# Expert layers issued in the order of a list scheduler inside the kernel, dense tails run in the next expert, float64 weights decoded in place

## The chip, the cores and the metric

The kernel runs on one core of a Trainium2 chip. The metric is device time in microseconds (us) of one launch; smaller is better. Engines are named as the profile names them: PE (TensorE matmuls, its weight loads PEld), DVE (VectorE), ACT (ScalarE), POOL (GpSimd), and SP, whose queue issues most DMAs.

## What is computed

Windowed attention, then a greedy assignment of 2304 tokens to 8 experts of 288 places each, two layers of the token's expert, and two dense layers:

```python
scores = np.where(mask, q @ k.T / 8 - slope * rel, -1e9)     # mask: 0 <= rel < 128; 4 batches, 8 heads, 576 rows, 64 wide
x = softmax(scores) @ v                                      # as 2304 rows of 512
for idx in np.argsort(-(x @ w_gate).flatten()):              # highest logit first
    tok, e = idx // 8, idx % 8
    if assigned[tok] < 0 and counts[e] < 288:
        assigned[tok] = e; counts[e] += 1
x[mask_e] = np.maximum(x[mask_e] @ w1[e], 0) @ w2[e]         # w1: 512x1024, w2: 1024x512, float32
h = x @ w_in                                                 # w_in: 512x2048, w_out: 2048x512, float64
out = np.maximum(0.01 * h, h) @ w_out
```

The assignment can be made one expert at a time: among the tokens left, the expert that is the first to be asked by 288 of them closes with these.

## The kernel before

Every float32 operand of a matmul is cut into two parts of a narrower form, high and low (`hh` and `hl`, `xh` and `xl`, `w1h` and `w1l`, and so on), and a product is three matmuls: high by high, low by high, high by low. ScalarE makes the high part by a copy; the low one is a subtraction on DVE or POOL (`Weights.split`).

Up to about 178.8 us the kernel runs the attention, and decodes 14 of the 16 tiles of `w_in` beside it. Float64 weights come as pairs of 32-bit words in a buffer `raw` (3 of them): ScalarE scales the upper words into a tile `wz`, DVE shifts the lower words in place and joins the two in `wz` (`Weights.fixed`), and the split into high and low reads `wz`. `raw` is free once the last joining step has read it. Then comes the assignment of the first expert (`Route.phase(0)`), and the loop over the eight experts:

- `X.gather` fetches the expert's 288 rows of x by three indirect DMAs from POOL's queue, and `X.turn` transposes them on PE into `xh` and `xl` (96 rows by three, two PSUM banks at a time).
- `X.moe` has 8 steps. A step loads its parts of w1 and w2 (SP queue), splits them, does 12 matmuls of the first layer into a bank `h`, the relu (ScalarE `hh`, DVE `hl`), and, one step later (lag 1), 12 of the second layer into four banks `acc`. At the end `acc` becomes `yh` and `yl`.
- `X.dense` has 16 steps of the same kind with resident weights and lag 2. Its leaky relu takes two ScalarE passes, a POOL subtraction (`lk`), a ScalarE copy (`hh`) and a POOL subtraction (`hl`). At the end `acc` is copied, transposed back on PE and scattered to the output rows by three indirect DMAs.

Beside them runs the assignment of the coming experts. For expert 1 it is `Route.phase(1)`, comparisons on DVE counted by matmuls. For experts 2 to 7 (`Late`) it is on DVE alone: a search of 11 rounds (`search`), each a scan of 1152 logits on each partition (`below`) and eight short steps on its result; `found` and `tokens`, which send a `line` of running counts through DRAM; and `listed`, three scans of that line that give `idx`, the rows to gather. `prepare` and `fetch` write the next candidates to DRAM and read them back.

The order of the work around all this was set by hand, in tables: at which dense step the next rows are gathered (`GATHER`) and turned (`TURN`), beside which steps a round of the search runs (`SEARCH`, `AHEAD`), which weights POOL splits (`POOL_W`), at which steps a dense tile is decoded (`IN_MOE`, `IN_DENSE`). `tc.issue_after(...)` ties a piece behind another instruction. On top of it the compiler's own scheduler moves instructions on each engine. At run time every engine works its queue in order.

Of the kernel before, what the change touches and what calls it, by code (L numbers as in the profile page):

```python
# [32 lines left out]
# engines of copies out of PSUM: A ScalarE, D VectorE; for weights by block, for an even and an odd unit  # L33
# [25 lines left out]
# shifts of the search by rows: digits of 3 bits, but the first of 2  # L59
# [40 lines left out]
class Attention:  # L100
    """Windowed attention of head pairs; leaves the rows of x in DRAM and the gate logits in SBUF.
# [298 lines left out]
class Route:  # L400
# [85 lines left out]
    def phase(s, i, ps, tb):  # L486
# [3 lines left out]
        def pst(shape):  # L490
            return ps.tile(shape, FT, name="T", bufs=tb)
# [16 lines left out]
        for rd, (bits, sh) in enumerate(rounds):  # L508
# [636 lines left out]
```

## Time and profile before

| | us |
|---|---|
| median of 3 runs | 962.7 |
| the runs | 963.95, 960.68, 962.70 |
| span of the profiled execution (the profile gives no other time of its own) | 959.1 |
| PE busy in it | 857.1 (89%) |
| DVE busy | 655.0 (68%) |
| ACT, POOL busy | 457.7 (48%), 389.8 (41%) |

The median is 3.6 us above the profiled span. Shares of busy time are means over stages with different limits, so the profile is read by stretches below. A stretch's line gives its length, then for each engine its busy time and the number of instructions, then the clock that was granted to PE as a share of 2.4 GHz, and the DMA engines' share and GB/s. A line of the timeline gives start, duration, engine, source line, operation, what is written and read, and in brackets the idle time of the engine before it with what ended it.

### The profile page before, as it was taken

What the parts mean: (1) busy time and instruction counts of PE and PEld (TensorE: products, weight loads), DVE (VectorE), ACT (ScalarE), POOL (GpSimd) and SP (SyncE); (2) the same over time, 40 slices, a digit from 0 to 9 for tenths busy, and PEclk for the clock granted to TensorE, in tenths of its full rate; (3) what the DMA queues carried; (4) which work ended last, traced back from release to release, by engine and by line L of the source; (5) the groups of instructions that cost most, each with busy time, mean ns of one, the idle gap of its engine ahead of it and who ended that gap; (6) DMA issues with size and microseconds to landing.
All of it is one profiled execution on the core that took longest, in us unless ns stands there. A gap on an engine that the chain in (4) does not pass through costs nothing.

```text
span 959.1 us, 18148 instructions
## 1 busy us (share of the span) xinstructions
PE 857.1 (89%) x6496; PEld 786.5 (82%) x6496; DVE 655.0 (68%) x1848; ACT 457.7 (48%) x1225; POOL 389.8 (41%) x430
## 2 busy tenths in 40 slices
PE   6999999669888989698988898889888999999995
PEld 5766766559778989598988898889888989999995
DVE  5789999768997797869767875886588525614200
ACT  5899888635545433343244324432443254344432
POOL 0021121210547635374467345734573441452353
PEclk9999999869988999799999998999899999999998
DMA  7567663146345301440404040404040312204000
GB/s 185 147 179 182 174 171 109 56 135 206 103 128 148 116 1 25 114 135 1 113 26 136 1 113 26 135 1 114 26 135 7 96 54 91 86 25 135 1 1 25
DMA packets 127578, 87.80 MB, mean 92 GB/s; under 512 B 70720, under 2 KB 112192, under 8 KB 127488
## 3 DMA queue, kind: packets, MB, share of 16 engines
q1 hardware_dynamic: 122944, 72.49, 27.3%
q0 software_dynamic: 4544, 14.16, 4.9%
q8 instruction: 51, 0.84, 0.3%
q14 instruction: 39, 0.32, 0.1%
HBM read 76.72 MB, written 9.91 MB: 90 GB/s over the span
## 4 chain that ended last, share of the span: by engine, by line
PE 36%; DVE 28%; issue 17%; POOL 10%; ACT 5%; DMA 3%; SPq 0%; POOLq 0%; DVEq 0%; ACTq 0%
PE acc L911 10%; PE h L921 8%; DVE below L678 6%; POOL lk L950 5%; PE X L281 4%; POOL hl L955 4%; PE T L247 3%; PE S L198 3%; DVE f L687 3%; ACT hh L954 2%; DVE th L700 2%; DVE wz L833 2%; PE T L158 1%; POOL xrow L866 1%; DVE next L676 1%
## 5 line engine op out<-in xcount | busy, mean ns | idle before, releaser
L950 POOL TENSOR_TENSOR lk<-lr,lk 128x288 f32<-128x288 f32 x128 | 108.5, 848 | 206.0 <-ACT lk L949 176.3
L955 POOL TENSOR_TENSOR hl<-lk,hh 128x288 fp32r<-128x288 f32 x128 | 106.0, 828 | 74.3 <-ACT hh L954 74.3
L954 ACT ACTIVATE hh<-lk 128x288 fp32r<-128x288 f32 x128 | 56.9, 444 | 165.5 <-POOL lk L950 165.3
L911 PE MATMUL acc<-hh,woh 128*128 128x288 f32 x512 | 97.7, 305 | 18.2 <-ACT hh L954 18.2
L911 PE MATMUL acc<-hh,wol 128*128 128x288 f32 x512 | 97.0, 304 | 0.0
L911 PE MATMUL acc<-hl,woh 128*128 128x288 f32 x512 | 96.5, 304 | 0.0
L911 PEld LDWEIGHTS acc<-hh,woh 128*128 128x128 f32 x512 | 79.4, 195 | 19.4 <-ACT hh L954 19.4
L921 PE MATMUL h<-yh,wih 128*128 128x288 f32 x512 | 94.8, 307 | 0.0
L921 PE MATMUL h<-yl,wih 128*128 128x288 f32 x512 | 92.2, 299 | 0.0
L948 ACT ACTIVATE lr<-h 128x288 f32<-128x288 f32 x128 | 52.0, 406 | 82.3 <-PE h L921 81.3
L921 PE MATMUL h<-yh,wil 128*128 128x288 f32 x512 | 89.9, 297 | 0.0
L921 PEld LDWEIGHTS h<-yh,wih 128*128 128x128 f32 x512 | 79.2, 196 | 0.9
L911 PEld LDWEIGHTS acc<-hl,woh 128*128 128x128 f32 x512 | 79.4, 196 | 0.4 <-POOL hl L955 0.3
L911 PEld LDWEIGHTS acc<-hh,wol 128*128 128x128 f32 x512 | 79.6, 195 | 0.1
L921 PEld LDWEIGHTS h<-yh,wil 128*128 128x128 f32 x512 | 76.4, 192 | 0.0
L921 PEld LDWEIGHTS h<-yl,wih 128*128 128x128 f32 x512 | 76.3, 190 | 0.0
L678 DVE TENSOR_SCALAR_CACHE_REDUCE below<-bc,th 128x1152 uint8<-128x1152 f32 x50 | 70.3, 1406 | 0.0
L795 DVE TENSOR_SCALAR_CACHE_REDUCE below<-lb,place 96x2304 uint8<-96x2304 f16 x18 | 47.0, 2608 | 34.2 <-DMA lb<-line 33.7
L232 ACT ACTIVATE P<-sc,mn 128x256 f32<-128x256 f32 (+1 forms) x144 | 68.3, 477 | 3.8 <-DVE mn L230 3.2
L911 PE MATMUL acc<-hl,w2h 128*128 128x288 f32 x256 | 52.9, 313 | 16.9 <-DVE hl L938 16.7
L810 POOL TENSOR_TENSOR w1l<-raw,w1h 128x512 fp32r<-128x512 f32 x36 | 47.7, 1325 | 32.4 <-ACT w1h L809 29.9
L809 ACT ACTIVATE w2h<-raw 128x512 fp32r<-128x512 f32 x64 | 40.3, 630 | 41.6 <-PE acc L911 30.7
(289 smaller groups left out, 1976.0 us busy)
## 6 DMA issues: line engine op xcount, KB each, us to landing
raw<-in_moe_w_dram SPq DMA_DIRECT2D x128, 256.0 KB, 3.0
raw<-in_moe_w_in_dram SPq DMA_DIRECT2D x16, 512.0 KB, 4.5
raw<-in_moe_w_out_dram SPq DMA_DIRECT2D x16, 512.0 KB, 4.1
qn<-in_q_dram SPq DMA_DIRECT2D x32, 128.0 KB, 2.5
kn<-in_k_dram SPq DMA_DIRECT2D x32, 128.0 KB, 3.0
vn<-in_v_dram SPq DMA_DIRECT2D x32, 128.0 KB, 2.4
xd<-rows POOLq DMA_DIRECT2D x16, 256.0 KB
bc<-cand SPq DMA_DIRECT2D x5, 576.0 KB, 5.4
```

The costliest lines, as they stand in the source:

```text
L232: nc.scalar.activation(P[:, x, w], sc[:, x, w], AF.Exp, bias=mn[:, x:x + 1], scale=-1.0, accum_out=acc)
L281: nc.tensor.matmul(xp[64 * h2:64 * h2 + 64, 128 * kb:128 * kb + n], V[:, kb, h2, :], t[:, n * h2:n * h2 + n], start=kb == 0, stop=kb == 3, ...
L678: V.tensor_scalar(junk, s.bc, s.thr.bitcast(FT), None, op0=OP.is_lt, op1=OP.add, accum_out=s.cl[:, 0:1])
L795: V.tensor_scalar(junk, lb, s.place[:, x:x + 1], None, op0=OP.is_lt, op1=OP.add, accum_out=at[:, x:x + 1])
L809: s.nc.scalar.activation(hi, raw, AF.Copy)
L810: (s.nc.gpsimd if pool else s.nc.vector).tensor_tensor(lo, raw, hi.bitcast(FT), op=OP.subtract)
L911: nc.tensor.matmul(acc[d], w[:, 128 * d:128 * d + 128], v, start=f == 0 and n == 0, stop=last and n == 2)
L921: nc.tensor.matmul(p, w[:, k], v[:, k], start=n == 0 and k == 0, stop=n == 2 and k == 3)
L948: nc.scalar.activation(r, p, AF.Relu)
L950: nc.gpsimd.tensor_tensor(t, r, t, op=OP.subtract)
L954: s.hh.append(nc.scalar.activation(hh, t, AF.Copy))
L955: s.hl.append((nc.gpsimd if pool else nc.vector).tensor_tensor(hl, t, hh.bitcast(FT), op=OP.subtract))
```

## The change

The loop over the experts no longer issues instructions. It writes down operations for a planner, `Plan`: each has an engine, a duration written in the code, a function that issues its instructions, the operations it comes after with a latency, the buffers it takes and gives back, and the time by which PE's train wants it. `Plan.run` then takes operations one at a time: for every engine it looks at those whose inputs and buffers are there, takes the engine on which something can start first, and on it the one wanted soonest; it issues it and sets the engine's clock on. The assignment is a thread of such operations (generators that `yield` engine and duration), which is wanted 60 or 80 us ahead of the list's use and otherwise fills gaps. `tc.manual_schedule()` keeps the order as issued. Operations with `alt` may go to DVE in place of POOL when they would be late. The hand-written tables are gone.

Besides, the expert layers have lag 2 from expert 1 on; the three last second-layer steps of the dense layers are handed on (`rest`) and issued among the next expert's first steps, and its output transposes after them; the turn uses one PSUM bank of its own (`tx`), the assignment and the outputs another (`to`); a one-element memset on POOL stands ahead of each scatter; float64 weights are decoded in `raw` itself, without `wz`, so that `raw` is held until the last split; `idx` and `ei` have five buffers instead of two; and the last tile of `w_in` is split ahead of the first assignment. In the attention nothing else is changed.

```diff
 class Weights:
-    nc.scalar.activation(z, high.bitcast(FT), AF.Copy, scale=2.0 ** -112)
-    nc.vector.tensor_scalar(low, low, 29, None, op0=OP.logical_shift_right)
-    nc.vector.scalar_tensor_tensor(x, x, 3, low, op0=OP.logical_shift_left, op1=OP.bitwise_or)
-    nc.vector.scalar_tensor_tensor(x, high, -2147483648, x, op0=OP.bitwise_and, op1=OP.bitwise_or)
+    def scale(e): nc.scalar.activation(v["high"].bitcast(FT), v["high"].bitcast(FT), AF.Copy, scale=2.0 ** -112)
+    def high(e): nc.vector.tensor_scalar(v["low"], v["low"], 29, None, op0=OP.logical_shift_right)
+    def both(e): nc.vector.scalar_tensor_tensor(v["low"], v["high"], 3, v["low"], op0=OP.logical_shift_left, op1=OP.bitwise_or)
+    def sign(e): nc.vector.scalar_tensor_tensor(v["low"], v["high"], -2147483648, v["low"], op0=OP.bitwise_and, op1=OP.bitwise_or)
+    def upper(e): nc.scalar.activation(hi, v["v"], AF.Copy)
+    def lower(e): (nc.gpsimd if e == "P" else nc.vector).tensor_tensor(lo, v["v"], hi.bitcast(FT), op=OP.subtract)
...
+class Plan:
+    LAT = 0.12
+    SLACK = 1.2
+    AHEAD = 9.0
+    WINDOW = {"T": 0.1, "V": 0.3, "A": 0.3, "P": 0.3, "S": 0.1}
...
+    def run(s, there, threads):
...
+            for o in s.ready:
+                t = s.start(o)
+                if t is None or o.eng == "T" and not o.owner and o.late > s.order[0].late + s.AHEAD:
+                    continue
+                for e in o.eng + (o.alt[0] if o.alt else ""):
+                    at = max(t, s.free[e])
+                    if e == o.eng or o.late - at < 1.0:
+                        found.setdefault(e, []).append((at, o.late, o))
+            e = min(found, key=lambda e: min(c[0] for c in found[e]))
+            first = min(c[0] for c in found[e])
+            at, _, o = min((c for c in found[e] if c[0] <= first + s.WINDOW[e]), key=lambda c: c[1])
...
+            o.end = s.free[e] = at + dur
+            if o.fn:
+                o.fn(e)
...
 class Experts:
+    MM, TR = .1325, .09
...
+    def fixed(s, src, shape, hi, lo):
+        raw = Hold("raw")
+        load = p("S", .5, fn[0], acq=[raw])
+        scale = p("A", .68, fn[1], [(load, 4.5)])
+        high = p("V", .45, fn[2], [(load, 4.5)])
+        both = p("V", .7, fn[3], [scale, high])
+        sign = p("V", .7, fn[4], [both])
+        upper = p("A", .63, fn[5], [sign])
+        lower = p("P", 1.32, fn[6], [upper], rel=[raw], alt=("V", .7))
...
+    def expert(s, i, x, reg, before):
+        for f in range(F1 // 128):
+            w = s.moe_weights(i, f, reg)
+            c, h, t = s.first(w[0][3], w[0][:2], w[0][2], lambda: (x["xh"], x["xl"]), (x["h"], x["l"]), x["hold"])
+            part = s.relu(c, h, t)
+            if f in (0, 1) and before:
+                before.pop(0)()
+            if f == 1 and i:
+                s.outputs()
+            pend.append((f, w[1], part))
+            if f >= 2 or (f == 1 and not i):
+                g, w2, pt = pend.pop(0)
+                s.second(g, False, w2[3], w2[:2], w2[2], pt, acc)
...
+        while pend:
+            rest.append(lambda p=pend.pop(0): s.dense_second(*p, out))
...
+    def route():
+        yield from R.second(first, ps, chosen[1], listed[1], ei, idx)
+        yield from LR.begin(first)
...
+        for i in range(2, NE):
+            if not last:
+                yield from LR.search()
+                yield from LR.found()
+            yield from LR.expert(last, chosen[i], ei)
+            yield from LR.tokens(last)
+            if i < NE - 2:
+                yield from LR.prepare()
+                yield from LR.fetch()
+            yield from LR.listed(listed[i], idx)
+    with tc.manual_schedule():
+        plan.run([listed[0], chosen[0], X.none], [Thread(route(), [(listed[1], 60.0)] + [(e, 80.0) for e in listed[2:]])])
```

What the planner makes of it is shown at three places, as the order of instructions on an engine. A row there is a source line, an operation, what it writes and reads, the size, and how many in a row.

PE between two experts in the middle of the run. Before (`acc<-hl,woh` ends the dense layers, `T<-ident,yh` and `h<-ident,yh` transpose the output, `h<-xh,w1h` begins the next expert):

```order
L911 MATMUL acc<-hl,woh 128x288
L979 MATMUL T<-ident,yh 96x128 x8
L979 MATMUL h<-ident,yh 96x128 x4
L921 MATMUL h<-xh,w1h 128x288 x4
L921 MATMUL h<-xh,w1l 128x288 x4
```

The output was transposed between the last dense matmul and the next expert's first. Now, between experts 2 and 3:

```order
L1280 MATMUL tx<-ident,xrow 128x96 x3
L1373 MATMUL acc<-hh,woh 128x288
L1373 MATMUL acc<-hh,wol 128x288
L1373 MATMUL acc<-hl,woh 128x288
L1354 MATMUL h<-xh,w1h 128x288 x8
L1354 MATMUL h<-xh,w1l 128x288 x8
L1354 MATMUL h<-xl,w1h 128x288 x8
L1373 MATMUL acc<-hh,woh 128x288
L1373 MATMUL acc<-hh,wol 128x288
L1373 MATMUL acc<-hl,woh 128x288
```

Two first-layer groups of the next expert stand ahead of the last dense matmuls; the transposes of the output (`to<-ident,yh`) follow later, one by one among its layers.

DVE where the list of an expert's rows is done (`below,at<-lb` are the scans of the line, `idx` the list, `below,cl<-bc` a scan of the next search, `xl` the low part of turned rows, `hl<-lk` a leaky step's low part). Before:

```order
L795 TENSOR_SCALAR below,at<-lb,place 96x2304 x3
L796 CAST idx<-at 96x3
L882 TENSOR_TENSOR xl<-T,xh 128x288 x4
L678 TENSOR_SCALAR below,cl<-bc,tk 128x1152
L680 STREAM_TRANSPOSE ct<-cl 128x32
```

The next search stood behind the four `xl` of the rows just listed. Now:

```order
L1242 TENSOR_TENSOR hl<-lk,hh 128x288
L1137 TENSOR_SCALAR below,at<-lb,place 96x2304 x3
L1140 CAST idx<-at 96x3
L988 TENSOR_SCALAR below,cl<-bc,tk 128x1152
L1242 TENSOR_TENSOR hl<-lk,hh 128x288
L995 STREAM_TRANSPOSE ct<-cl 128x32
```

The search goes on at once, and the `xl` stand among its later rounds.

SP's queue in the first expert (`in_moe_w_dram` are an expert's weights, `in_moe_w_out_dram` and `in_moe_w_in_dram` the dense ones). Before, the last of the expert's weights and what follows:

```order
L824 DMA raw<-in_moe_w_out_dram 128x1024
L889 ISA
L889 DMA raw<-in_moe_w_dram 128x4x128
L890 ISA
L890 DMA raw<-in_moe_w_dram 128x512
L889 ISA
L889 DMA raw<-in_moe_w_dram 128x4x128
L890 ISA
L890 DMA raw<-in_moe_w_dram 128x512
L824 DMA raw<-in_moe_w_out_dram 128x1024 x8
L824 DMA raw<-in_moe_w_in_dram 128x4x256
```

Some dense tiles were loaded among the expert's weights. Now:

```order
L1306 DMA raw<-in_moe_w_dram 128x4x128
L1309 ISA
L1309 DMA raw<-in_moe_w_dram 128x512
L1177 DMA raw<-in_moe_w_out_dram 128x1024 x3
L1609 TENSOR_LOAD ei
L1609 ISA x2
L1177 DMA raw<-in_moe_w_out_dram 128x1024 x6
L912 DMA flat<-lm 128x4x8
```

Two tiles of `w_out` stand ahead of the expert's weights; the other fourteen and the two of `w_in` come behind all of them.

## Rows read from the trace of the kernel before

**Rows 1.** Stretches of each expert (E0 to E7) and the end.
```profile
208.40:316.00 107.60, 95.20 (x732) 90.69 (x732) 88.84 (x180) 54.82 (x121) 45.36 (x44) 0.91 0.48 140
316.00:414.40 98.40, 86.08 (x605) 83.86 (x604) 79.57 (x229) 36.26 (x85) 51.07 (x53) 0.93 0.23 62
414.40:510.00 95.60, 84.74 (x609) 82.41 (x608) 71.63 (x188) 36.13 (x86) 51.87 (x55) 0.97 0.26 74
510.00:605.40 95.40, 84.58 (x600) 82.72 (x600) 71.19 (x187) 34.95 (x84) 49.65 (x52) 0.94 0.22 64
605.40:700.40 95.00, 84.22 (x598) 82.34 (x597) 70.72 (x188) 34.80 (x84) 50.68 (x53) 0.95 0.24 69
700.40:786.90 86.50, 79.10 (x579) 77.49 (x578) 55.93 (x139) 34.08 (x82) 45.87 (x49) 0.98 0.25 74
786.90:867.00 80.10, 79.02 (x598) 78.22 (x597) 34.45 (x64) 34.97 (x84) 31.55 (x38) 1.00 0.24 73
867.00:947.60 80.60, 80.60 (x608) 80.05 (x607) 16.07 (x29) 32.49 (x77) 29.65 (x36) 1.00 0.09 29
947.60:959.10 11.50, 1.43 (x12) 1.00 (x10) 0.75 (x2) 1.60 (x3) 2.76 (x3) 0.78 0.17 51
```

**Rows 2.** Timeline of PE: a count of E0's assignment, and two dense steps.
```profile
251.80 0.61 PE L518 MATMUL T<-rt_oh,cmp 128*31 128x8 bf16 x18 [1.62 <-DVE cmp L471]
...
686.83 0.69 PE L921 MATMUL h<-yh,wih 128*128 128x288 f32 x4
...
690.01 0.43 PE L921 MATMUL h<-yh,wih 128*128 128x288 f32 x2
```

**Rows 3.** Waits of PE, 208.4 to 947.6: total, times, longest.
```profile
PE acc L911 <- ACT hh L954: 18.2, 5, 4.9
PE acc L911 <- DVE hl L938: 16.7, 16, 2.1
PE T L879 <- DVE xl L882: 10.3, 4, 4.7
PE T L979 <- DVE yh L975: 7.5, 3, 2.5
PE T L879 <- DMA xrow<-xd,idx: 4.4, 1, 4.4
```

**Rows 4.** Timeline of DVE in E2: list scans, turn, three search scans.
```profile
470.11 2.61 DVE L795 TENSOR_SCALAR_CACHE_REDUCE below<-lb,place 96x2304 uint8<-96x2304 f16 x1 [5.34 <-DMA lb<-line]
...
487.75 0.82 DVE L882 TENSOR_TENSOR xl<-T,xh 128x288 fp32r<-128x288 f32 x2 [9.52 <-ACT xh L881]
...
494.49 1.41 DVE L678 TENSOR_SCALAR_CACHE_REDUCE below<-bc,th 128x1152 uint8<-128x1152 f32 x1
...
497.26 1.41 DVE L678 TENSOR_SCALAR_CACHE_REDUCE below<-bc,th 128x1152 uint8<-128x1152 f32 x1
...
500.85 1.41 DVE L678 TENSOR_SCALAR_CACHE_REDUCE below<-bc,th 128x1152 uint8<-128x1152 f32 x1
```

**Rows 5.** Groups of DVE in E2: busy us, mean ns of one.
```profile
L938 DVE SCALAR_TENSOR_TENSOR hl<-h,hh 128x288 fp32r<-128x288 f32 x8 | 3.6, 445 | 1.9 <-issue 1.9
...
L810 DVE TENSOR_TENSOR w1l<-raw,w1h 128x512 fp32r<-128x512 f32 x1 | 0.7, 686 | 0.0
```

**Rows 6.** Timeline of SP's queue: eight tiles of w_out in a row.
```profile
230.27 27.63 SPq L824 DMA_DIRECT2D raw<-in_moe_w_out_dram  x8
```

**Rows 7.** Groups of ACT in E0: strided scale, copy of packed words.
```profile
L830 ACT ACTIVATE wz<-raw 128x512 f32<-128x512 f32 x17 | 11.5, 674 | 8.0 <-DVE wol L810 2.7 <-DMA raw<-in_moe_w_out_dram 2.6 <-DVE wz L832 1.6
L809 ACT ACTIVATE woh<-wz 128x512 fp32r<-128x512 f32 x15 | 9.4, 629 | 7.2 <-DVE wz L833 7.0
```

**Rows 8.** Groups of DVE in E0's expert layers, 208.4 to 238.5.
```profile
L833 DVE SCALAR_TENSOR_TENSOR wz<-raw,wz 128x512 int32<-128x512 int32 x4 | 2.7, 680 | 0.0
```

**Rows 9.** Groups of DVE in E0's dense layers, 238.5 to 316.
```profile
L833 DVE SCALAR_TENSOR_TENSOR wz<-raw,wz 128x512 int32<-128x512 int32 x13 | 15.2, 1169 | 0.0
L832 DVE SCALAR_TENSOR_TENSOR wz<-wz,raw 128x512 int32<-128x512 int32 x13 | 12.1, 933 | 1.7 <-ACT wz L830 1.4
```

More of the change, by code (lines that the diff above doesn't have):

```diff
@@ new lines, in __init__, with pe, copy, minus @@
+        s.at = 9.0
+        s.wi_there, s.wo_there = {}, {}
+    def pe(s, dur, fn, after, **k):
+        o = s.plan.op("T", dur, fn, after, late=s.at, **k)
+        s.at += dur
+        return o
+    def copy(s, e, o, i):
+        if e == "A":
+            s.nc.scalar.activation(o, i, AF.Copy)
+        else:
+            s.nc.vector.tensor_copy(o, i)
+    def minus(s, e, o, a, b):
+        (s.nc.gpsimd if e == "P" else s.nc.vector).tensor_tensor(o, a, b, op=OP.subtract)
+    def warm(s, n):
+        def go(e):
+            for _ in range(n):
+                p = s.ps.tile([128, 512], FT, name="h", bufs=2)
+                s.nc.tensor.matmul(p, s.wih[0][:, 0, :128], s.wih[0][:, 0, :512], start=True, stop=True)
+        s.plan.op("T", 3.8, go, late=0.0)
@@ new lines, in second, with mm, by_part, go @@
+    def second(s, f, last, w, wops, hold_w, part, acc):
+        nc = s.nc
+        def mm(d, n):
+            a, b = w(), part["get"]()
+            x, y = ((0, 0), (1, 0), (0, 1))[n]
+            nc.tensor.matmul(acc["p"][d], a[x][:, 128 * d:128 * d + 128], b[y], start=f == 0 and n == 0, stop=last and n == 2)
+        def by_part(n):
+            def go(e):
+                if f == 0 and n == 0:
+                    acc["p"] = [s.ps.tile([128, CAP], FT, name="acc", bufs=4) for _ in range(4)]
+                for d in range(4):
+                    mm(d, n)
+            return go
+        def by_bank(d):
+            def go(e):
+                for n in range(3):
+                    mm(d, n)
+            return go
+        rel = [part["hold"]] + ([hold_w] if hold_w else [])
+        after = [[wops[0], part["h"]], [wops[1]], [part["l"]]]
+        if last:
+            prev, acc["done"] = acc["prev"], []
+            for d in range(4):
+                prev = [s.pe(3 * s.MM, by_bank(d), sum(after, []) + prev, rel=rel)]
+                acc["done"].append(prev[0])
+        else:
+            prev = acc.get("prev", [])
+            for n in range(3):
+                prev = [s.pe(4 * s.MM, by_part(n), after[n] + prev, rel=rel, acq=acc["hold"] if f == 0 and n == 0 else ())]
+            acc["prev"] = prev
@@ new lines, in tile_attention_moe_mlp, with value @@
+    first = era.enter_context(tc.tile_pool(name="first", bufs=1))
+    LR = Late(tc, keep, dram, R, L)
+    idx, ei = [idx0], [ei0]
+    listed = [plan.op(None, 0.0) for _ in range(NE)]
+    chosen = [plan.op(None, 0.0) for _ in range(NE)]
+    X.warm(8)
+    rest = None
+    for i in range(NE):
+        reg = [None, []]
+        def value(e, i=i, reg=reg):
+            reg[1].append(nc.sync.value_load(ei[i][0:1, 0:1], min_val=0, max_val=NE - 1))
+        reg[0] = plan.op("S", .5, value, [chosen[i]])
+        x = X.turn(i, X.gather(i, [listed[i]], lambda i=i: idx[i]))
+        if i:
+            X.idx_out, X.is_last = (lambda i=i: idx[i - 1]), False
+        rest = X.expert(i, x, reg, rest)
```

869 lines of the change are left out of this document (592 added, 277 removed).

## The prediction

> **What bounds the kernel now.** I read the stretches first, one for each expert's two layers with the two dense layers after them; I call them E0 to E7. TensorE (PE) does the same matmuls in each, yet they last from 107.6 us down to 80.1 [rows 1]. In E6 it is busy for 79.02 of 80.10 us at a granted clock of 1.00, which is 2.4 GHz: that is what an expert costs when nothing holds PE up, and I take 79 as its price. The matmul train says the same: from one first-layer group to the next, 24 matmuls with 288 columns, 686.83 to 690.01, are 3.18 us [rows 2], or 0.1325 each; an expert has 24 blocks of 24 of them, 576, so 76.3 us, and the rest is transposes. E0 also holds the matmuls of the second assignment, 18 in 0.61 us for each of six rounds (one of them in [rows 2]) and some smaller ones, about 6 us: its price is 85.
>
> So the eight stretches should cost 85 + 7 x 79 = 638 us, and cost 739.2 (208.40 to 947.60). The 101 us over that lie in E0 to E5, and the waits of PE tell how [rows 3]: 18.2 us for `hh` of the dense layers, 16.7 for `hl` of the expert layers, 10.3 for `xl` of the turned rows, 7.5 for the copy out of the accumulators, 4.4 for gathered rows. With smaller ones that is some 65 us. The rest is the clock: a stretch at 0.93 spent about 14% of its time at 1.2 GHz, always behind such waits. E6 and E7, with the same layers but hardly any search, have neither. What differs is VectorE (DVE): 88.84 us busy in E0, 79.57 in E1, some 71 in E2 to E4, 34 and 16 in the last two [rows 1]. DVE carries the assignment of tokens, whose chain for one expert has to end before the next expert's rows are gathered. In its timeline a round of the search takes 2.77 us (494.49 to 497.26) or, where a few of its small steps are held up, 3.59 (497.26 to 500.85); DVE then waits 5.34 us for the list's line, and 9.52 us for `xl`, in which it does nothing of the search [rows 4]. The bound is thus PE in E6 and E7, and the assignment in turn with PE in E0 to E5: each waits for the other.
>
> **The change, part by part.**
>
> *Dense tails and transposes moved.* The three last second-layer steps stand behind two first groups of the next expert, and the output transposes among its matmuls. No PE work is added. What goes is the wait for the copy (7.5 us) and for the last `hh` (a part of 18.2). The cover is 24 matmuls at 0.1325, 3.2 us, more than the longest copy wait of 2.5 [rows 3].
>
> *Expert layers at lag 2.* A second-layer group now comes two steps behind its first, so `hl` has 3.2 us more than before; the longest wait for it was 2.1 us [rows 3]. I take the 16.7 us as gone wherever DVE keeps up.
>
> *The search runs on behind the list.* This decides. In the new DVE order the next search follows the list of places directly, where it used to stand behind `xl`; the 9.52 us are filled. But the order also says how much DVE has to do before it may release PE. Between the first `xl` of one turn and that of the next it has 15 search scans in E1, 13 in E2, 12 in E3, 11 in E4 and 4 in E5, where each had 11. DVE is an in-order queue, so these stand before the next turn. From E2's 71.6 us [rows 1], with 3.2 us a round (the mean of 2.77 and 3.59), 0.686 for a weight split and 0.445 for an `hl` [rows 5]:
> E1: 71.6 + 4 rounds (12.8) + 3 splits more (2.1) + the last dense tile's decoding (3.0, four steps of 0.5 to 0.9) + 2 `hl` (0.9) = 90.4, of which a little falls into E0's last steps: 89.
> E2: 71.6 + 2 x 3.2 + 4 x 0.686 + 8 x 0.445 = 84.3: 84.
> E3: 71.6 + 3.2 + 7 x 0.686 + 4 x 0.445 = 81.4: 81.5.
> E4: 71.6 + 9 x 0.686 + 5 x 0.445 = 80.0, with PE's 79 beside it: 81.
> E5 needs 7 rounds fewer, so PE bounds it: 79 and 1.5 for four turns through a single PSUM bank instead of two: 80.5. E6 and E7: 80 each, as now.
>
> *E0: the second assignment beside the expert layers, decoding in place.* DVE's 88.84 us lose 9 weight splits (25 stood on it, by the two orders 16 do now) and two copies, 7.2 us, and gain 7 dense `hl`, 3.2: 84.9, and it starts on the assignment while the first rows are still on their way. The other limit is the three load buffers. A tile now holds its buffer until its last split; before, until the last decoding step. Before, eight tiles in a row left the queue in 27.63 us [rows 6], 3.45 a tile. Now 16 tiles (14 of w_out, 2 of w_in) come behind the expert's weights, from about 232: 16 x 3.45 = 55 to 287, and some 8 to land, decode and split the last, so 295, and the tails after that: E0 ends near 298, at 90 instead of 107.6. In place, every step walks over every other word. Some did before: ScalarE's scale reads strided words in 0.674 us where its copy of packed ones takes 0.629 [rows 7], 7% more, and DVE's last step, strided in one operand, ran in 0.68 undisturbed [rows 8]. A strided split on GpSimd is shown by no row. Its ends are the 7% (0.09 us) and the double of its 1.3 us, for twice the words walked over, which over three buffers would be 0.43 a tile, 4 us for the 9 tiles that go there. I take the near end, 0.
>
> *Elsewhere.* One split (ScalarE 0.63, GpSimd 1.3) moves ahead of the first assignment, where GpSimd is idle: nothing. In the attention the order shifts by a few rows and load buffers are held longer; PE is close to full there, and I allow 2 us either way. A one-element memset ahead of each scattered row waits where the scatter waited: nothing. On SP's queue the rows' list and candidates stand behind weight loads that wait for a buffer, as before. The end after the last matmul stays at 11.5 us [rows 1].
>
> *Sum.* 90 + 89 + 84 + 81.5 + 81 + 80.5 + 80 + 80 = 666, against 739.2: 73.2 less. The profiled span is 959.1; 885.9 remain. The median of the runs, 962.7, is 3.6 over that span, and I carry it on: **889 us**.
>
> **A rule against it.** The decoding's last step took 680 ns beside E0's expert layers, which leave GpSimd almost free, and 1169 beside its dense layers, whose activation GpSimd works on [rows 8, 9]. The Trainium skill (SBUF — State Buffer, "SBUF: two separate sides") states that VectorE and GpSimd share a port pair under an exclusive lock: a VectorE instruction with two SBUF inputs waits out a whole GpSimd one, and the reverse. The rows agree. By that rule, packing both engines tighter lengthens both, and the third rival below is what comes of it; my sum takes the disturbed prices as they stand, since in E2 to E4 GpSimd loses splits to DVE.
>
> **The rivals.**
> 1. *PE bounds everything.* DVE is disturbed less, a round costs 2.77, and 15 rounds fit. Then E0 is 85 to 87 and the others 79.5: 643, 96 less, so 959.1 - 96 + 3.6 = 867. For it: the undisturbed rounds. Against: DVE's count in E1 is still 15 x 2.77 = 41.6 and the rest 42, so 84.
> 2. *The chain stays the bound.* If each expert's assignment still takes the 95 us it takes now, whatever stands between, E1 to E4 stay at 95 and E5 at 86, and E0 and the tails are all: 90 + 4 x 95 + 86 + 160 = 716, so 939. Against: 15 us of each such stretch are DVE's waits [rows 4].
> 3. *The shared port and the buffers.* The disturbed 1169 and 933 ns [rows 9] hold for all 17 tiles of E0, the last tile comes no sooner, E0 stays at 107, and E1 at 95: 107 + 95 + 84 + 81.5 + 81 + 80.5 + 160 = 689, so 912.
> 4. *Slower: a fixed order of short waits.* PE's queue now alternates groups of two chains, so each waits for the later one. If the list's places fit badly and every one of the 24 steps of an expert waits 0.6 us (the mean wait for `hl` is 16.7 / 16 = 1.0), that is 192 x 0.6 = 115 us on 638: 753, so 208.4 + 753 + 11.5 + 3.6 = 977. It decides from 0.53 us a step, where the 101 us are eaten up. Against: in E6 and E7 steps of the same kind wait for nothing.
>
> **Numbers.** My forecast has 0.58, the rivals 0.16, 0.05, 0.13 and 0.06; 0.02 is for no change at all. About 0.3% is what a measurement of this kernel tells from no change. All but the fourth and the last are faster: 0.92; same 0.02; slower 0.06. The forecast's own spread is 876 to 902 (E1 between 83 and 93, the buffers, the attention). Eight in ten reach over the first rival's middle and the third's: 864 to 914.
>
> **What would show it.** Right: E0 near 90 and E1 near 89 with DVE busy for over nine tenths of both, E3 to E7 near 80 at a granted clock of 1.00, the wait for `yh` gone and `hl` under 4 us in total, the last scan of the search some 20 us ahead of its gather by E4. A first-order error would be DVE idle in E1 with PE waiting (a chain that waits for GpSimd or the queue), or E2 to E4 above 90. The forecast fails if the sum over E1 to E5 is above 440 or below 400, or if the attention moves by over 4 us.

## The result and the profile after

The changed kernel takes 938.3 us (median of 4 runs, 934.03 to 942.21), the kernel before 961.7 beside it: a ratio of 0.9755, with a 95% interval of 0.9718 to 0.9791. That is faster by 23 us, where the forecast was 889 (864 to 914). The direction was right, the size a third of what was said.

The profiled execution has a span of 935.4. Its stretches are cut at the first matmul of each expert's layers, so what an expert hands on and runs behind that matmul counts with the next one. Three second-layer steps (36 matmuls) are handed on, but the planner issues most of them ahead of the next expert all the same: by the trace 3 to 12 of the 36 stand behind its first matmul (12 between E0 and E1 and between E6 and E7), 1.6 us at 0.1325 each at most. The row ahead of E0 runs from the point where it began before. Columns as in [rows 1]:

```profile
208.40:213.90 5.50, 2.75 (x29) 2.44 (x29) 5.29 (x12) 1.64 (x4) 1.04 (x1) 0.58 0.35 103
213.90:321.40 107.50, 93.18 (x675) 87.15 (x675) 85.22 (x161) 51.54 (x112) 48.83 (x44) 0.91 0.44 131
321.40:419.90 98.50, 85.75 (x612) 82.93 (x612) 87.78 (x240) 37.28 (x89) 50.91 (x55) 0.96 0.28 83
419.90:508.00 88.10, 82.15 (x599) 78.91 (x598) 81.09 (x222) 35.12 (x84) 40.00 (x44) 1.00 0.26 75
508.00:591.20 83.20, 80.53 (x596) 78.41 (x595) 73.18 (x200) 34.77 (x85) 39.11 (x44) 1.00 0.27 79
591.20:678.80 87.60, 83.49 (x606) 81.13 (x605) 74.96 (x202) 35.31 (x85) 36.12 (x42) 0.98 0.25 75
678.80:761.70 82.90, 81.03 (x598) 78.72 (x598) 62.14 (x150) 35.37 (x85) 37.03 (x42) 1.00 0.26 77
761.70:842.60 80.90, 80.55 (x602) 79.20 (x601) 15.72 (x26) 34.88 (x85) 43.84 (x50) 1.00 0.22 68
842.60:923.80 81.20, 80.56 (x604) 79.67 (x602) 12.41 (x21) 32.41 (x79) 39.25 (x46) 1.00 0.09 28
923.80:935.40 11.60, 1.79 (x12) 1.01 (x10) 1.14 (x2) 1.22 (x3) 2.93 (x5) 0.75 0.17 51
```

Against [rows 1], E0 with 107.5 and E1 with 98.5 are as long as before, and E0 starts 5.5 later. The whole gain lies in E2 to E5: 341.8 in place of 372.5 by those rows. Four cuts of [rows 1], at 510.00, 605.40, 786.90 and 867.00, miss the first matmul, which stands at 508.63, 604.91, 790.03 and 870.69. Cut there, E2 to E5 took 375.6 before, so 33.8 are gained, and E6 and E7 took 80.7 and 76.9, so 4.5 are lost. In E2 to E5 PE's idle time falls from 39.9 us to 14.6 and its busy time from 335.7 to 327.2, at a granted clock of 1.00 in place of 0.96. Against the forecast E0 is 17.5 too long, E1 9.5, E2 4.1, E4 6.6, E3 and E5 to E7 together 6.2; with the late start of 5.5 that is the 49 us between 889 and 938.

The waits of PE from 208.4 to 923.8 (total, times, longest) answer to [rows 3]:

```profile
PE tx L1280 <- DVE xl L1242: 11.1, 5, 4.2
PE h L1354 <- DVE f L1004: 6.8, 1, 6.8
PE acc L1373 <- DVE hl L1242: 3.4, 5, 1.0
PE acc L1373 <- ACT hh L1438: 3.2, 5, 1.4
PE h L1354 <- DVE hl L1414: 2.9, 2, 2.4
```

The waits for the copies are gone, as said; those for the dense layers' `hh` fall from 18.2 us to 3.2, and those for the expert layers' `hl` from 16.7 to 2.9. What is left is for the most part DVE: `xl` as much as before, and one wait of 6.8 us at the start of E1.

**E0.** Two views tell why it did not shrink. The first is SP's queue, the dense tiles' loads (start, duration of the issues, line, count):

```profile
239.60 39.81 SPq L1177 DMA_DIRECT2D raw<-in_moe_w_out_dram  x9
...
297.56 5.40 SPq L1177 DMA_DIRECT2D raw<-in_moe_w_out_dram  x2
...
309.37 0.34 SPq L1177 DMA_DIRECT2D raw<-in_moe_w_out_dram  x1
```

The sixteen tiles leave from 239.60 to 309.37, one in 4.65 us, not in 3.45 from 232 on. The second is E0 cut at 245:

```profile
213.90:245.00 31.10, 29.64 (x217) 28.05 (x217) 18.04 (x41) 11.84 (x24) 10.68 (x8) 0.85 0.45 135
245.00:321.40 76.40, 63.54 (x463) 59.10 (x462) 67.17 (x120) 39.70 (x89) 38.16 (x36) 0.94 0.44 130
```

DVE is busy for 18.04 of the first 31.10 us: the tiles that it could decode stand behind all of the expert's weights. From 252 to 311 its timeline has hardly a gap. PE, busy for 63.54 of 76.40, waits 4.9 us for the last tiles, 4.2 for `xl` behind a stop of DVE at 311, and 2.3 for a step of the assignment. The granted clock adds to it: 0.55 in E0's first 10 us (in the 5.50 us ahead PE was busy for 2.75), 1.00 from 223.9 to 303.9, and 0.72 in the last 17.5, among those waits. So PE is busy for 93.18 us with work priced at 85, less the 1.6 handed on: 9.8 more, where 0.45 of 10 and 0.28 of 17.5 would be 9.4, an estimate. The 14.3 us of idle PE and these 9.8 are what E0 has over its price. DVE's 85.22 us in all are what the forecast worked out, 84.9. They only don't begin when the stretch does.

**E1.** The timeline of DVE at its start, with PE's wait from the same stretch:

```profile
323.15 1.41 DVE L988 TENSOR_SCALAR_CACHE_REDUCE below<-bc,tk 128x1152 uint8<-128x1152 f32 x1
...
328.19 1.41 DVE L988 TENSOR_SCALAR_CACHE_REDUCE below<-bc,th 128x1152 uint8<-128x1152 f32 x1
...
331.85 1.41 DVE L988 TENSOR_SCALAR_CACHE_REDUCE below<-bc,th 128x1152 uint8<-128x1152 f32 x1
...
333.66 0.44 DVE L1414 SCALAR_TENSOR_TENSOR hl<-h,hh 128x288 fp32r<-128x288 f32 x1
```

```profile
334.25 1.30 PE L1354 MATMUL h<-xh,w1h 128*128 128x288 f32 x4 [6.81 <-DVE f L1004]
```

The low part `hl`, whose high part was ready at 324.2, stands behind three rounds of the search. It frees the bank that PE's third group writes, and PE waits 6.81 us (the profile names the instruction that it sees last, a step of the round). The planner put it there: the search, wanted 80 us ahead, was the more urgent. Behind the wait the granted clock was 0.66 from 331.4 to 341.4, so the one wait cost some 9 us, an estimate (6.81, and 0.34 of the 7.15 us for which PE is busy there). PE's waits in E1 come to 12.7 us in all, 3.0 of them for `xl`.

### The profile page after: what moved, and what is told of

Same layout as the page of the kernel before. It is cut to its first block, busy times and chain, and to the rows that moved or that the text cites. A ratio compares the mean times of both kernels' runs of the same rounds, so it can differ in the third digit from the quotient of the medians.

```text
span 935.4 us, 18237 instructions
## 1 busy us (share of the span) xinstructions
PE 853.8 (91%) x6496; PEld 775.7 (83%) x6496; DVE 665.7 (71%) x1878; ACT 456.9 (49%) x1225; POOL 372.4 (40%) x423
## 4 chain that ended last, share of the span: by engine, by line
PE 49%; DVE 28%; ACT 7%; issue 6%; DMA 5%; POOL 4%; SPq 0%; POOLq 0%; DVEq 0%; ACTq 0%
PE h L1354 17%; PE acc L1373 17%; DVE below L988 4%; PE X L269 3%; ACT P L220 3%; PE T L235 3%; PE S L186 2%; DMA raw<-in_moe_w_dram 2%; DVE raw L1200 1%; DMA cand<-lm 1%; DVE raw L1196 1%; DVE f L1004 1%; PE T L146 1%; DVE hl L1242 1%; DMA bc<-cand 1%
## 5 line engine op out<-in xcount | busy, mean ns | idle before, releaser
L1242 POOL TENSOR_TENSOR hl<-lk,hh 128x288 fp32r<-128x288 f32 x95 | 78.5, 826 | 57.8 <-ACT hh L1438 57.6
L1354 PE MATMUL h<-yh,wih 128*128 128x288 f32 x512 | 91.4, 301 | 4.6 <-ACT lk L1431 2.8
L1373 PE MATMUL acc<-hh,wol 128*128 128x288 f32 x512 | 94.8, 300 | 0.9 <-POOL wol L1206 0.6
L1242 POOL TENSOR_TENSOR w1l<-raw,w1h 128x512 fp32r<-128x512 f32 x40 | 52.4, 1310 | 90.1 <-ACT w1h L1317 89.6
L1354 PE MATMUL h<-yh,wil 128*128 128x288 f32 x512 | 87.5, 296 | 0.8 <-POOL wil L1206 0.8
L1354 PEld LDWEIGHTS h<-yh,wih 128*128 128x128 f32 x512 | 75.1, 188 | 8.9 <-ACT lk L1431 4.8
L1373 PEld LDWEIGHTS acc<-hh,wol 128*128 128x128 f32 x512 | 77.4, 191 | 1.9 <-POOL wol L1206 1.1
L1317 ACT ACTIVATE w1h<-raw 128x512 fp32r<-128x512 f32 x64 | 40.3, 630 | 71.4 <-PE h L1354 33.6
L1431 ACT ACTIVATE lk<-h 128x288 f32<-128x288 f32 x128 | 51.1, 407 | 24.4 <-DVE hl L1242 14.7
L1206 POOL TENSOR_TENSOR wil<-raw,wih 128x512 fp32r<-128x512 f32 x13 | 17.1, 1315 | 106.1 <-ACT wih L1203 95.0
```

The source lines that it names most:

```text
L1242: (s.nc.gpsimd if e == "P" else s.nc.vector).tensor_tensor(o, a, b, op=OP.subtract)
L1317: nc.scalar.activation(v[x][0], v["r"][x], AF.Copy)
L1354: nc.tensor.matmul(t["p"], a[x][:, k], b[y][:, k], start=n == 0 and k == 0, stop=n == 2 and k == 3)
L1373: nc.tensor.matmul(acc["p"][d], a[x][:, 128 * d:128 * d + 128], b[y], start=f == 0 and n == 0, stop=last and n == 2)
L1431: nc.scalar.activation(v["t"], t["p"], AF.Relu, scale=-0.01)
```

## The experiments

Times are medians, each with its ratio to the kernel before, measured beside it, and the 95% interval; lengths of E0 to E7 are those of the one profiled execution, which in six of the runs is their slowest (by 7 us above the median in the run with the search at 70 us). The cuts of code are shortened to the lines that matter. The changed kernel stands at 938.3, 0.9755 (0.9718 to 0.9791).

### E0: buffers, GpSimd, or DVE's amount

A fourth load buffer, in the memory that the search takes over later:

```diff
-    t = v["t"] = s.raw()
+    t = v["t"] = s.rawx() if f in (2, 3, 4, 8, 12) else s.raw()     # rawx: one buffer in the pool "first"
```

> A fourth load buffer for five dense tiles of the first expert. Now 16 dense tiles leave the queue in 69.8 us (239.60 to 309.37), 4.65 each, and PE waits for the last ones. Buffers as the bound: with four the tiles leave at about 3.5 us, the last at 295 or before, E0 (first matmul of expert 0 to first of expert 1, now 107.5) falls to about 95, the time from 938 to about 926. DVE as the bound (it works back to back from 252 to 311, with its steps lengthened beside GpSimd): the same work stays behind the same queue, E0 gains at most the 5 us by which the first extra tiles start sooner, 933 to 938.

Measured: 927.3, 0.9624 (0.9602 to 0.9646). DVE does 21.69 us in place of 18.04 by 245, and E0 is 104.1 in the profile, though that execution, with a time of 933.9, is the slowest of its six (923.8 to 933.9). Most of the gain that buffers promised is there, less of it in E0 than was said. The tiles' rate did not improve: 14 of them leave from 241.58 to 303.71, one in 4.8 us. What is different is that two leave sooner, at 201.98 and 236.49, and that DVE starts on them; I take that as what helped, and no run shows it alone.

GpSimd's subtraction `lk` left out in expert 0:

```diff
-    nc.gpsimd.tensor_tensor(v["t"], v["r"], v["t"], op=OP.subtract)
+    if i: nc.gpsimd.tensor_tensor(v["t"], v["r"], v["t"], op=OP.subtract)
```

> Leaves out GpSimd's subtraction of the leaky relu in the first expert's dense layers, 16 operations of 1.06 us; the order of all else stays. Lengthening by GpSimd: the decoding's three DVE steps (0.55, 0.91 and 1.01 us a tile) come back towards 0.42, 0.69 and 0.69, about 0.67 us for each of 17 tiles, and E0 falls by about 11 us, the time to about 927. Buffers or order as the bound: the steps may be shorter, but E0 falls by 3 us at most, 935 to 938.

Measured: 933.1, 0.9699 (0.9665 to 0.9732), E0 99.1. The three decoding steps of DVE in E0, in the changed kernel and then here (count, busy us, mean ns):

```profile
L1200 DVE SCALAR_TENSOR_TENSOR raw<-raw 128x512 int32<-128x512 int32 x17 | 17.2, 1010 | 0.3
L1196 DVE SCALAR_TENSOR_TENSOR raw<-raw 128x512 int32<-128x512 int32 x17 | 15.5, 913 | 0.8
L1192 DVE TENSOR_SCALAR raw<-raw 128x512 int32<-128x512 int32 x17 | 9.3, 545 | 0.0
```

```profile
L1196 DVE SCALAR_TENSOR_TENSOR raw<-raw 128x512 int32<-128x512 int32 x17 | 14.9, 879 | 0.8
L1200 DVE SCALAR_TENSOR_TENSOR raw<-raw 128x512 int32<-128x512 int32 x18 | 14.3, 795 | 0.3
L1192 DVE TENSOR_SCALAR raw<-raw 128x512 int32<-128x512 int32 x17 | 7.6, 450 | 0.0
```

Together they come half the way back, from 2.47 us a tile to 2.12, where undisturbed ones take 0.69, 0.69 and 0.41; E0 falls by 8.4, between the two theories. So GpSimd's work is part of DVE's length. The run also takes a step out of the relu's own chain, and how much of the 8.4 is due to that isn't told apart.

DVE's decoding left out:

```diff
-    def high(e): nc.vector.tensor_scalar(v["low"], v["low"], 29, None, op0=OP.logical_shift_right)
+    def high(e): pass                               # so too both and sign
```

> Leaves out DVE's three decoding steps of the 18 tiles in the expert loop (the shift and the two joining ones, some 42 us of DVE), and takes the scaled upper words as weights; loads, splits and the order of all else stay. DVE's decoding as the cause of E0's excess: E0 from 107.5 to 92 or less, the time to 923 or less. Load buffers and the place of the loads in the queue as the cause: the tiles still come one behind the other at 3.5 us or more, E0 100 or more, 930 to 935.

Measured: 924.1, 0.9624 (0.9606 to 0.9642). The first two stretches:

```profile
212.10:306.30 94.20, 86.57 (x676) 83.22 (x675) 47.46 (x110) 51.39 (x112) 45.43 (x44) 0.95 0.50 150
306.30:407.60 101.30, 88.89 (x612) 86.61 (x611) 86.60 (x238) 37.57 (x89) 50.20 (x55) 0.91 0.28 83
```

With 38 us less on DVE, E0 loses 13, to 94.2, between the two theories, and E1 takes 3 of them back. Its tiles still leave only from 234.50 to 294.87, one in 4.02 us. DVE's decoding is the larger part of E0's excess. The rest is hardly the tiles: PE waits 1.2 us for them, 4.8 for `xl` at E0's end, and the clock is 0.95.

Decoding out of place, which undoes that part of the change for 11 tiles:

```diff
-    nc.scalar.activation(high, high, AF.Copy, scale=2.0 ** -112)
+    z = s.more.tile([128, 512], FT, name="wz", bufs=2)
+    nc.scalar.activation(z, high, AF.Copy, scale=2.0 ** -112)
```

> Eleven of the 16 dense tiles of the first expert are decoded into a tile of their own, as before the change, so a load buffer comes free at the last decoding step and not at the last split, some 3.5 us of its 14 sooner. Decoding in place as the cost: the tiles leave the queue at about 3.6 us in place of 4.65, E0 falls by about 10, the time to about 928. DVE as the bound: the queue moves, E0 doesn't, 936 to 938.

Measured: 935.9, 0.9730 (0.9687 to 0.9773): no difference that can be told. The queue, which both theories had moving, didn't move: the sixteen tiles leave from 241.14 to 310.36, one in 4.61 us, though a load buffer is free a split sooner. With the fourth buffer it was 4.8, without the decoding 4.02: that points to DVE's pace more than to the load buffers. Decoding in place costs nothing to speak of, by its longer hold as by its strided words; beside the attention GpSimd's split takes 1298 ns from `raw` and took 1278 from `wz`.

The wait at the change of pools, 311 to 315, taken out:

```diff
-    s.cl = sb.tile([128, 32], FT, name="cl")        # so too res, ends, place
+    s.cl = s.keep.tile([128, 32], FT, name="cl")
```

> Three small tiles and the list of places are kept outside the pool that takes the first pool's memory, so DVE and GpSimd don't wait at 311 for the candidates' DMA (DVE stood 3.54 us, GpSimd 5.12, PE 4.21 behind them). If that stall is on the path: E0 shorter by about 4 us, 934. If the last dense tiles set the end of E0 anyway: nothing, 938.

Measured: 937.5, 0.9761 (0.9734 to 0.9787). What E0 gains, at 103.4, E1 loses, at 102.2: that wait was hidden, or came back elsewhere.

### E1 to E5: the search on DVE

Each round of the first search with a second scan:

```diff
     V.tensor_scalar(junk, s.bc, s.thr, None, op0=OP.is_lt, op1=OP.add, accum_out=s.cl[:, 0:1])
+    V.tensor_scalar(junk, s.bc, s.thr, None, op0=OP.is_lt, op1=OP.add, accum_out=jk)
```

> Adds a second scan of 1.41 us to each of the 11 rounds of the search for expert 2, which runs beside expert 1; its result isn't used. DVE (search in turn with PE) as the bound of E1: E1 from 98.5 to about 114, the time to about 954. PE as the bound of E1, the search in DVE's gaps: E1 longer by 5 us at most, up to 943.

Measured: 948.3, 0.9855 (0.9811 to 0.9899). E1 grows to 107.9, E2 to 92.2: of 15.5 us of scans the whole takes 10. Most of the added work lies on the path, and a third of it finds room. The scans lengthen the search's chain as much as DVE's amount, so this run doesn't tell these two apart.

The search held back behind the third `hl` of expert 1, and the search wanted 70 us ahead in place of 80:

```diff
+    yield "S", .01, {"after": [(X.mark, .1)]}      # X.mark: hl of the third step of expert 1
     yield from LR.search()
```

```diff
-    [(listed[1], 60.0)] + [(e, 80.0) for e in listed[2:]]
+    [(listed[1], 60.0)] + [(e, 70.0) for e in listed[2:]]
```

> The search for expert 2 starts only behind the low part of the third step of expert 1, which stood behind three of its rounds while PE waited 6.81 us for the bank that it frees. If this is what lengthens E1: the wait and the slow clock after it go, E1 from 98.5 to about 90, the time to 930. If the assignment's chain is the bound in E1: the search ends some 10 us later, PE waits for the list or the turned rows at E1's end instead, E1 stays at 98 to 105, 938 to 945.

> The planner wants the search 70 us ahead of the list's use and not 80; so in expert 1 more low parts and splits stand ahead of search rounds, and the search ends later. The search's urgency as the cause of E0's and E1's excess: PE's 6.81 us wait goes and E0 and E1 together fall by 7 us or more, 931 or less. DVE's amount of work as the bound: what PE doesn't wait for at E1's start it waits for at its end; E0 and E1 together within 3 us of 206, 935 to 942.

Measured: 944.5, 0.9816 (0.9776 to 0.9856), with E1 at 104.8; and 944.0, 0.9810 (0.9790 to 0.9831), with E0 at 101.3 and E1 at 108.0, 209.3 for the two where the changed kernel has 206.0. Both are some 6 us slower, with intervals that touch the change's. In the first the wait came back at the next place. DVE, GpSimd and PE there:

```profile
340.44 3.07 DVE L992 TENSOR_TENSOR next<-tk,fb 128x1 int32<-128x1 int32 x1
...
351.63 0.45 DVE L1414 SCALAR_TENSOR_TENSOR hl<-h,hh 128x288 fp32r<-128x288 f32 x1
```

```profile
339.77 1.28 POOL L1242 TENSOR_TENSOR w1l<-raw,w1h 128x512 fp32r<-128x512 f32 x1
341.01 1.27 POOL L1242 TENSOR_TENSOR w2l<-raw,w2h 128x512 fp32r<-128x512 f32 x1
342.23 1.25 POOL L1242 TENSOR_TENSOR w1l<-raw,w1h 128x512 fp32r<-128x512 f32 x1
```

```profile
352.23 1.30 PE L1354 MATMUL h<-xh,w1h 128*128 128x288 f32 x4 [11.82 <-DVE next L992]
```

Six rounds now stand ahead of the `hl` of 351.63. So holding the search back moves PE's wait and doesn't shorten it: 17.8 us of waits in E1 in place of 12.7. The rows show one thing more: a step on one number per partition, 128x1, took 3.07 us. It began inside the first of three GpSimd splits in a row and ended with the third (343.51 and 343.48).

The planner given the measured prices:

```diff
-    both = p("V", .7, fn[3], [scale, high])
-    sign = p("V", .7, fn[4], [both])
+    both = p("V", .91, fn[3], [scale, high])
+    sign = p("V", 1.01, fn[4], [both])
```

> The planner is given what the decoding takes on the chip (0.55, 0.91 and 1.01 us on DVE in place of 0.45, 0.7 and 0.7; splits 0.82 on DVE and 1.40 on GpSimd in place of 0.7 and 1.32) and makes another order from it. An order made for wrong durations as the cause: E0 and E1 together shorter by 5 us or more, 932 or less. DVE's amount of work as the cause: another order of the same work, 935 to 942.

Measured: 936.7, 0.9728 (0.9697 to 0.9758). Another order of the same work, no gain.

Work moved from DVE to GpSimd and ScalarE, alone and with the fourth buffer:

```diff
-    o = s.plan.op("P", 1.32, lower, [u], rel=[raw], alt=("V", .7))
+    o = s.plan.op("P", 1.32, lower, [u], rel=[raw], alt=None if 1 <= i <= 5 else ("V", .7))
```

> From expert 1 on all weight splits of experts 1 to 5 stay on GpSimd, and the copies of the outputs go to ScalarE: DVE loses some 3 to 8 us of work in each of E1 to E4. DVE's amount as the bound of E1 to E4: these four shorter by 3 us each, 923 to 928. PE or the chain's latencies as the bound: GpSimd's splits come later, PE waits for them, 936 to 942.

> The fourth load buffer of the first run, the change of the run before, and the dense layers' low parts on GpSimd alone. If the two gains add: 912 to 918. If GpSimd's greater load lengthens DVE's steps as much as DVE is relieved: 925 to 930.

Measured: 946.5, 0.9854 (0.9812 to 0.9897), and 951.2, 0.9906 (0.9874 to 0.9937): slower than either theory had it, and the second loses the buffer's gain and more. In the first, E1 falls to 93.9, but E3 and E4 grow to 89.3 and 94.1, and E1's DVE has fewer instructions (233 for 240) and is busy for longer (88.33 for 87.78). Splits went to GpSimd and copies to ScalarE at once, so what each did alone is open.

GpSimd's subtraction left out in experts 1 and 2:

```diff
-    nc.gpsimd.tensor_tensor(v["t"], v["r"], v["t"], op=OP.subtract)
+    if i not in (1, 2): nc.gpsimd.tensor_tensor(v["t"], v["r"], v["t"], op=OP.subtract)
```

> Leaves out GpSimd's subtraction of the leaky relu in experts 1 and 2 in place of expert 0, 16 operations of 0.82 us in each; the order of all else stays. In E1 DVE's steps take 17.8 us more than their undisturbed prices, nearly all of it while a GpSimd operation runs. GpSimd's share as a cost of E1 and E2: a quarter of it goes with a quarter of GpSimd's work, E1 and E2 together shorter by 6 us or more, 932 or less. The order of the queue (search ahead of the low parts) or PE as the bound: 2 us or less, 936 to 940.

Measured: 930.0, 0.9668 (0.9646 to 0.9689). E1 and E2:

```profile
320.80:414.50 93.70, 85.65 (x612) 83.90 (x612) 82.06 (x240) 37.77 (x89) 38.27 (x39) 0.94 0.30 87
414.50:502.10 87.60, 83.15 (x599) 80.24 (x598) 74.20 (x222) 35.06 (x84) 26.89 (x28) 0.98 0.27 75
```

With 13 us less on GpSimd in each, the same 240 and 222 DVE instructions take 82.06 for 87.78 and 74.20 for 81.09. So the lengthening of DVE's steps is there in E1 and E2 too. The stretches gain less than DVE does: E1 is 4.8 us shorter and E2 0.5, together a little short of the 6 named. This run, too, shortens the relu's chain.

Last, GpSimd's work left as it is, and three operands of the search's small steps moved to PSUM, into the unused part of the bank of the turned rows:

```diff
-    s.fb = P.tile([128, 1], I32, name="fb")
+    s.fb = s.side[:, 288:289].bitcast(I32)          # side: the tx bank; so too next and n
```

> Three small tiles of the search's rounds lie in PSUM, in the unused part of the turned rows' bank, so that three of its steps a round have at most one operand in SBUF; the order stays. In the changed kernel these steps (128x1 and 128x14) take 0.15 us alone and 0.45 to 0.68 beside GpSimd, 15 us too much over all rounds. If the pair of ports that VectorE and GpSimd share is the cause: they take 0.15 to 0.2 each time, DVE loses 2 to 4 us in each of E1 to E4, the time falls to about 929. If the lengthening has another cause, or the rounds run in gaps: the steps stay long or the time stays, 936 to 940.

> The same with the fourth load buffer of the first run (927.3 alone). If the two gains add: 918 to 921. If E1's end is set by the splits and not by the search: 926 to 928.

Measured: 930.6, 0.9669 (0.9644 to 0.9693), and with the buffer 918.2, 0.9552 (0.9527 to 0.9576). The four steps in E1, in the changed kernel and then in the first of the two:

```profile
L992 DVE TENSOR_TENSOR next<-tk,fb 128x1 int32<-128x1 int32 x13 | 5.0, 382 | 0.0
L1021 DVE SCALAR_TENSOR_TENSOR th<-dx,next 128x1 int32<-128x1 int32 x12 | 3.9, 326 | 0.3
...
L1004 DVE TENSOR_SCALAR f<-n 128x14 f32<-128x14 f32 x14 | 3.0, 217 | 0.4
...
L1024 DVE SCALAR_TENSOR_TENSOR fb<-dx,fb 128x1 int32<-128x1 int32 x13 | 2.6, 198 | 0.0
```

```profile
L1007 DVE TENSOR_SCALAR f<-tx 128x14 f32<-128x14 f32 x13 | 2.2, 169 | 0.3
...
L1027 DVE SCALAR_TENSOR_TENSOR tx<-dx,tx 128x1 int32<-128x1 int32 x13 | 2.1, 164 | 1.0 <-PE tx L1283 0.6
L995 DVE TENSOR_TENSOR tx<-tk,tx 128x1 int32<-128x1 int32 x12 | 1.9, 156 | 0.0
L1024 DVE SCALAR_TENSOR_TENSOR th<-dx,tx 128x1 int32<-128x1 int32 x12 | 1.8, 154 | 0.3
```

(`tx` is the bank that now holds `next`, `fb` and `n`.) 52 steps of 14.5 us became 50 of 8.0, with the same order and GpSimd's work as it was. In the timelines from 321 to 680, `next` took 0.60 us on average where a GpSimd operation ran beside it and 0.15 alone, and `f` 0.39 and 0.17; in this run `next` takes 0.16 and `f` 0.17 either way. DVE's busy time falls by 7.1 us in E1, 5.5 in E2, 3.7 in E3 and 6.2 in E4, the stretches by 4.1, nothing, 0.6 and 3.1.

The two gains add, and with the buffer this kernel is 4.5% faster than the one before and some 20 us faster than the change; E0 and E1 are 99.2 and 90.4 (why E0 falls by 8.3, when the buffer alone took 3.4 off it in its profile and this step alone left it at 107.9, isn't shown):

```profile
213.90:313.10 99.20, 87.61 (x675) 83.62 (x675) 88.46 (x164) 52.48 (x112) 48.53 (x42) 0.95 0.47 138
313.10:403.50 90.40, 84.43 (x613) 81.98 (x612) 77.96 (x237) 36.50 (x89) 50.74 (x55) 0.98 0.30 89
```

### The tails and the lag

```diff
-    rest.append(lambda p=pend.pop(0): s.dense_second(*p, out))
+    s.dense_second(*pend.pop(0), out)
```

```diff
-    if f >= 2 or (f == 1 and not i):
+    if f >= 1:
```

> The last three second-layer steps of the dense layers run at the end of their own expert again; the output transposes stay among the next expert's steps. Tails as a main gain: PE waits at each of seven borders for the last low part and the copies of the accumulators, 2 us or more each, with the slow clock behind it: 952 to 960. Tails as a small one (the border is filled with turned rows and first groups anyway): 940 to 945.

> Expert layers of experts 1 to 7 with lag 1 in place of 2. Lag as a main gain: PE waits for the low part of each relu, 1 us or more in 16 or more places as it did before: 950 or more. Lag as a small one (the list scheduler finds DVE free there): 939 to 943.

Measured: with the tails at home 933.8, 0.9731 (0.9675 to 0.9788), within the interval of the change; with lag 1 946.0, 0.9828 (0.9784 to 0.9873), 8 us slower. Both miss their theories: the first is below either, the second between the two. Handing on the tails gives nothing here; since the planner left at most 12 of the 36 matmuls behind the border, there was little to take back. Lag 2 gives about 8.

The fourth buffer and the tails at home together:

> The fourth load buffer and the tails at their own expert's end, both of which were faster than the change alone. If the gains add (11 and 4): 923. If the fourth buffer's gain already holds what the tails at home gave: 927.

Measured: 929.6, 0.9675 (0.9654 to 0.9696): like the buffer alone, not below it.

## Why the prediction was wrong, step by step

1. *PE's price of 79 to 81 an expert:* right. E6 and E7 take 80.9 and 81.2, at a clock of 1.00. The E6 that it was read from is cut 3 us early; from first matmul to first matmul it took 80.7.
2. *E0, 90:* wrong, and the largest miss. DVE's amount was right (84.9 against 85.22). What failed is "16 x 3.45 = 55 to 287, and some 8 to land": the tiles started at 239.60, not 232, and took 4.65 each, at the pace of a DVE that is full from 252; and DVE stood for 13 of the first 31 us. The 3.45 was misread besides: between eight tiles there are seven gaps, and from the first's start (230.27) to the eighth's (257.57) they are 3.9 each. I had counted DVE's sum and the queue's sum apart and taken the larger. They stand one behind the other: without the decoding E0 is 13 shorter. The slow clock, some 9.8 us, had no term beside E0's price of 85. The tile prices were those of before, as I had said; without GpSimd's subtraction E0 is 8.4 shorter.
3. *E1, 89, and E2, 84:* DVE's sums were near (90.4 against 87.78, 84.3 against 81.09), but the stretches lasted 10.7 and 7.0 us longer than DVE's busy time. An in-order DVE that waits for PE, in turn with a PE that waits for DVE, needs more than the larger of the two. The forecast made that point of the kernel before and dropped it for the kernel after. In E1 one wait of 6.81 us for a `hl` behind the search, with the slow clock after it, is about as large as the miss of 9.5. The added scans show that most of the search's work there lies on the path.
4. *The disturbed prices kept as they stand:* wrong. "In E2 to E4 GpSimd loses splits to DVE" did not make it better. Taking GpSimd's subtraction away in two experts gave 8 us (930.0), taking operands of the small steps out of SBUF 8 (930.6), and moving splits onto GpSimd and copies onto ScalarE cost 8.
5. *E3 to E5, 81.5, 81 and 80.5:* 83.2, 87.6 and 82.9. E4's excess is not settled: 4 us of PE's waits, 2.4 of them for `xl`, and a clock of 0.98.
6. *Tails, 7.5 and a part of 18.2, and lag 2, 16.7:* the waits went, but with the tails at home the time is the same, and the lag is worth 8. "The three last second-layer steps stand behind two first groups" is not what the planner made of it: one step at most does. Where PE waits for DVE anyway, a wait removed can turn up elsewhere.
7. *Decoding in place, 0:* right, for the strided words and for the longer hold.
8. *The attention, 2 either way:* 3 late by the first list (DVE writes it at 201.88, before at 198.89), 2.5 more before E0's first group. Not tried apart; in the runs above, which leave the attention as it is, E0 starts between 212.1 and 215.6.

The second rival gave 939, and the time is 938, but not by its mechanism: E2 to E4 did not stay at 95. The third, shared port and buffers, had E0 at 107 and E1 at 95, and came nearest for these two (107.5 and 98.5); it had the later experts too short. By the tests named ahead, the sum over E1 to E5 is 440.3, just beyond the upper bound of 440, and E0's start moved by 5.5 us, beyond the 4 allowed to the attention.

Of the gain of 23 us, 8 go when the lag goes; the rest, the order of turns, transposes and search, was not taken apart. Of the 49 us missed, the 5.5 before E0 and the 6.6 of E4 have no run that shows their cause.

## What to carry to other kernels

An engine's busy sum is a floor for a stretch and not its length: DVE's sums were right within 3.3 us in E0 to E2, and the stretches were 22, 11 and 7 us longer than them. Ask at which moment its first work can be there, what holds the buffers that bring it, and which low-priority work stands ahead of a small step that frees another engine. A scheduler that fills gaps by urgency can place long work there by its own plan, and the one run with better prices didn't cure it. Where GpSimd and VectorE both run, cut what they contend for before moving work from the one to the other.

## What the runs showed of the hardware

A VectorE step can be held for the whole of a GpSimd operation, however small it is. In E1 of the changed kernel, DVE and then GpSimd:

```profile
326.96 1.19 DVE L1019 TENSOR_TENSOR th<-tk,fb 128x1 int32<-128x1 int32 x1
...
329.53 1.09 DVE L992 TENSOR_TENSOR next<-tk,fb 128x1 int32<-128x1 int32 x1
...
333.19 0.15 DVE L992 TENSOR_TENSOR next<-tk,fb 128x1 int32<-128x1 int32 x1
```

```profile
326.87 1.27 POOL L1242 TENSOR_TENSOR w2l<-raw,w2h 128x512 fp32r<-128x512 f32 x1
329.35 1.26 POOL L1242 TENSOR_TENSOR w1l<-raw,w1h 128x512 fp32r<-128x512 f32 x1 [1.21 <-ACT w1h L1317]
```

The two long steps end with the split beside them (328.15 and 328.14, 330.62 and 330.61); the same step alone takes 0.15. Held are steps with two operands in SBUF (`next`, `th`, the splits) and some with one (`f`, some copies, the decoding's shift); the scans (1.41 us each time), the transposes and the steps that read PSUM are not. That fits the Trainium skill (SBUF — State Buffer, "SBUF: two separate sides"), which states that VectorE and GpSimd have one port pair under an exclusive lock, held for the whole instruction, for VectorE operations in a two-port mode or with two SBUF inputs. The cure by a PSUM operand (0.38 to 0.16 us for `next`) agrees with that condition, since such a step has no two SBUF inputs. The 128x1 step that waited past two splits to the end of a third goes beyond it. The Trainium skill also says that moving work between the two "might not help" (Perfetto Trace Analysis, "Optimizing Scalar/DVE Operations"). The two runs that did so agree, in that they lost 8 and 13 us against the change, though they moved copies to ScalarE as well.
